# One group of products moved in the forward and in the backward chain of a recurrent attention block

## The chip, the cores and the metric

The kernel runs on one core of one Trainium2 chip. The metric is the device time of one launch in microseconds. The profile names the engines PE (TensorE matmul), PEld (TensorE weight load), DVE (VectorE), ACT (ScalarE), POOL (GpSimd) and SP (SyncE, which issues most of the transfers).

## The reference

The reference computes the output and all gradients of a block that multiplies a memory-augmented attention with a gated unit. The attention walks over 64 segments of 32 tokens. Each segment sees 8 memory rows and its own 32 rows, and its own memory output is the memory of the next segment:

```python
for s in range(n_seg):                       # 64 segments, one after the other
    h = concatenate([mem, xs[s]], axis=1)    # 8 memory rows + 32 rows, width 640
    q, k, v = h @ Wq, h @ Wk, h @ Wv         # 32 heads of 128
    p = softmax(where(mask, q @ k.T * scale, -1e9))
    o = (p @ v) @ Wo
    mem = o[:, :8]                           # feeds the next segment
    outs.append(o[:, 8:])
out = x + s * silu(swiglu(layernorm(x)))     # s: the outs; swiglu with w1, w3, w2
# returned: out and the gradients to x, mem0, Wq, Wk, Wv, Wo, w1, w3, w2
```

Since the memory passes from segment to segment, both the forward pass and the gradient pass hold a chain of 64 steps that can't run side by side.

## The kernel before

The program has five stages one after the other: the gated unit forward, the forward chain (`recurrence`, 390 to 1810 us of the profile with the work around it), the backward chain (`phase4_Abwd`, to 2890 us), the weight gradients of the attention (to 4370 us), and the gated unit backward.

**Chain and fillings.** In each chain, `chain(t, gap)` writes the work of step t that hangs on the memory rows: projections of few rows by `packed_half` (line L306; four column groups of the PE array at a time), a softmax, and output products by `packed_out` (L325). The other 32 rows of a segment don't hang on the chain. Their work is cut into units: three segments (a tile `tl`) by four heads (`qd`), eight units a tile, so three, three and two units a step (`SPL`). At named points the chain calls `gap("W0")`, `gap("W1")`, ..., `gap("G6")`, and what is called there, `at(f, t, i)`, writes operation `f` of unit i of step t into the instruction stream. The order on each engine is the written order (`in_order`): no scheduler moves an instruction of a chain, and each engine works through its list front to back. PE's sum of the chain goes to banks bA, bB, bC of PSUM; the units share five buffers with the tag `x`.

**The fold.** `packed_out` leaves its result in four parts. `fold_add` sums them: ACT copies two parts (`fup`, L334), DVE adds (`fsum`, L336, in two halves). `fold_turn` (L352) then turns the sum on PE, and DVE copies it into the input of the next step (`hx`). Between the last product and the turn PE has only what gaps G4 (backward) or G5 (forward) give it. The table `WARM` names gaps in which PE also gets dummy products of 512 columns whose result nobody reads (L915 forward, L1430 backward).

**Forward unit.** Its scores and softmax run in gaps G1 to G4, `turn_p` (L840) turns the probabilities, `norm` (L831 to L833) normalizes them on POOL and stores them. `pv` forms the value products: `pv_mm` on PE (four products of 96 columns, L860, in the steps that keep them, and four of 128, L863), `pv_turned` copies the first on ACT and stores them from ACT's queue (`xoT`, L872), `pv_rows` copies the second on ACT (`xv`, L92) and stores the rows from POOL's queue (L880). The `pv` of the first unit of step t-1 stands in gap W0 of step t, between the two key halves and the first query half. Key turns of a third unit (`kprep`, L743) stand there too in two of three steps. The first query half goes into bank bA, from which DVE copies the first key half (`stg`, L90).

**Backward unit.** `turn` turns what was loaded, `dprob` (L1337, L1338) forms the gradient of the probabilities, `dsoft` (DVE, L1350 and L1353) that of the scores, and `gmem` forms what the memory rows of keys and values get from the other rows: eight products of 24 columns (L1365, L1366), two copies on ACT (`gks`, L1369), a store from POOL's queue (`GXP`, L1371). `gmem_ld` adds `ld_next`, four loads from SP's queue into the buffer that the products have just read. The step's end is `packed_out` of `gkT` with WkT (48 products), gap G3, `packed_out` of `gqT` with WqT (64 products), `fold_add`, gap G4, `fold_turn`, gap G5. In 59 of the 64 steps, t = 62 to 4, there are units.

Of the kernel before, what the change touches and what calls it, by code (L numbers as in the profile page):

```python
# [554 lines left out]
def recurrence(k, W0, W4, Wv, Wk_, Wq, Wo, own, ps, banks):  # L555
    nc, tc = k.nc, k.tc
    D, DC, S, H, HD, T = k.D, k.DC, k.S, k.H, k.HD, k.T
    with tc.tile_pool(name="achain", bufs=1) as ch, \
# [5 lines left out]
        WARM = dict(G2=1, G3=2, G5=2)  # L564

        def ride_ld(t):
            x0 = k.NB0 + 24 * t
            b, sub = t // 4, t % 4
            if sub == 0 and x0 < S:
                w = min(96, S - x0)  # L570
                rt = ch.tile([P, DC, 96], BF16, name="ride", tag="ride")
                turned_load(k, rt[:, :, 0:w], k.XN[x0:x0 + w, :])
                rides[b] = (rt, w)
# [164 lines left out]
        def kprep(tl, qd, eng='s'):  # L738
            ns, nm, nx, n = k.geo(tl)
            kr = uu.pop(("kr", tl, qd))  # L740
            pt = ps.tile([P, 4, nx], BF16, name="kpt", tag="x", bufs=5)
            for j in range(4):
                nc.tensor.transpose(pt[:, j, :], kr[0:nx, j * P:(j + 1) * P], k.ident[0:nx, 0:nx])  # L743
            dst = kTs[tl % 2][:, qd * 4:qd * 4 + 4, 0:n].rearrange("p h (s c) -> p h s c", c=40)[:, :, :, 8:40]
            k.copy(dst, pt[:].rearrange("p h (s c) -> p h s c", c=32), eng=eng)

        def ld(w, tl, qd, eng=nc.sync):
            nm = k.geo(tl)[1]
            c0 = qd * 512
            r = fl.tile([120, 512], BF16, name=f"x{w}", tag=f"x{w}", bufs=2 if w == "q" else 3)  # L750
            if qd >= (5 if w == "q" else 2):
                ns, nm, nx, n = k.geo(tl)
                g0 = 512 * (qd % 2)
                eng.dma_start(r[nx:n], k.QVM[3 * tl:3 * tl + ns, :, qd // 2, "qv".index(w), g0:g0 + 512].rearrange("t r c -> (t r) c"))
            else:
                k.load_m(r, tl, w, c0, c0 + 512, eng)
            k.load_x(r, 0, k.x_src(tl, w, c0, c0 + 512), eng)
            uu[w, tl, qd] = r
# [84 lines left out]
        def oride_ld(t):  # L843
            if 0 <= t - k.OT0 < k.NO:
                r = ch.tile([P, H, 24], BF16, name="oride", tag="oride")
                nc.sync.dma_start(r[:], k.OTX[t - k.OT0])
                uu["o", t] = r
# [43 lines left out]
        batch = {}  # L891
# [26 lines left out]
        def FILL(g, t, at, kbatch):  # L918
            kb = kbatch.get(t, ())
            if g == "W0":  # L920
                oride_ld(t)
                at(pv, t - 1, 0)
                for u in kbatch.get(t - 1, ())[2:]:
                    kprep(*u)
            elif g == "W1":
                at(pv_mm, t - 1, 1)
                at(pv_turned, t - 1, 1)
                at(turn_p, t - 1, 2)
                at(lambda a, b: ld("v", a, b), t - 1, 2)
            elif g == "V0":  # L930
                at(pv_rows, t - 1, 1)
            elif g == "W2":
                ride_ld(t + 1)
                for u in kb[0:2]:
                    ld_k(*u)
            elif g == "G1":
                oride(t)
                at(pv_mm, t - 1, 2)
                at(turn_q, t, 2)
                for i in range(2):  # L940
                    at(lambda a, b: ld("q", a, b), t + 1, i)
            elif g == "G2":
                at(lambda a, b: pv_turned(a, b, qo=nc.gpsimd), t - 1, 2)
                at(pv_rows, t - 1, 2)
                for i in range(3):
                    at(scores, t, i)
                at(soft_max, t, 0)
                for i in range(2):
                    at(lambda a, b: ld("v", a, b), t, i)
            elif g == "G3":  # L950
                at(lambda a, b: soft_exp(a, b, 0, 2), t, 0)
                at(soft_max, t, 1)
            elif g == "G4":
                at(lambda a, b: soft_exp(a, b, 2, 4), t, 0)
                at(lambda a, b: soft_max(a, b, True), t, 2)
                at(norm, t, 0)
                at(soft_sub, t, 2)
                for u in kb[0:2]:
                    kprep(*u, 'v')
                for u in kb[2:]:  # L960
                    ld_k(*u)
                at(soft_exp, t, 1)
                at(norm, t, 1)
                at(soft_exp, t, 2)
            elif g == "G5":
                at(turn_p, t, 0)
                at(turn_q, t + 1, 0)
                at(turn_q, t + 1, 1)
                at(lambda a, b: ld("q", a, b), t + 1, 2)
            elif g == "G6":  # L970
                at(turn_p, t, 1)
                at(norm, t, 2)
        tail = [u for t in sorted(batch) if t >= T for u in batch[t]]
        fA, fB, fC = [b_[:] for b_ in (bA, bB, bC)]
# [54 lines left out]
        batch = {t: b for t, b in batch.items() if t < T}  # L1029
# [53 lines left out]
def phase4_Abwd(k, out2, W0, W4, WT, own, ps, banks):  # L1083
# [20 lines left out]
    with tc.tile_pool(name="gst", bufs=1) as st, tc.tile_pool(name="gchain", bufs=1) as ch, \  # L1104
# [25 lines left out]
        WARM = dict(G4=1)  # L1130
# [247 lines left out]
        batch = {}  # L1378
# [14 lines left out]
        def gap_of(t):  # L1393
            def at(f, tt, i0, i1=None):
                b = batch.get(tt, ())
                for u in b[i0:i0 + 1 if i1 is None else i1]:
                    f(*u)

            def gap(g):
                if g == "W0":  # L1400
                    ride_ld(t - 1)
                    at(turn, t, 0)
                elif g == "W1":
                    at(turn, t, 1)
                    at(gmem_ld, t + 1, 2)
                elif g == "G1":
                    at(dprob, t, 0)
                elif g == "G2":
                    at(dprob, t, 1)
                    at(turn, t, 2)  # L1410
                    at(dsoft, t, 0)
                elif g == "G3":
                    if t > 0:
                        load_xp(t - 1)
                    at(dsoft, t, 1)
                    at(gmem_ld, t, 0)
                elif g == "G4":
                    at(dprob, t, 2)
                elif g == "G5":
                    at(gmem_ld, t, 1)  # L1420
                elif g == "G6":
                    at(dsoft, t, 2)
                if t == 0 and g == "G1":
                    fetch.append(Fetch(k, W0))
                if t == 0 and g in ("G1", "G2"):
                    fetch[0].to(2 if g == "G1" else 3)
                if t == 0 and g == "G3":
                    fetch[0].w(0)
                for i in range(WARM.get(g, 0)):
                    nc.tensor.matmul((bA if g in ("W1", "G2") else bB)[:], k.ident[:], WqT[:, 0, 0:512], start=True, stop=True)  # L1430
            return gap
        todo = pro + todo
# [859 lines left out]
```

## Time and profile before

| what | value |
|---|---|
| median of 3 runs | 4680.79 us (4674.91 to 4681.3) |
| profiled execution | 4678.86 us, its span 4677.0 us |
| mean granted PE clock | 0.987 |
| PE busy, whole span | 4454.0 us (95%) |
| PEld, DVE, ACT, POOL busy | 2818.5, 2244.2, 1588.7, 2104.2 us |
| forward chain, 390 to 1810 us | PE 1324.05 us busy, clock 0.98, DMA share 0.62 |
| backward chain, 1810 to 2890 us | PE 1030.86 us busy, clock 0.99, DMA share 0.71 |

The span is one execution as the hardware profiler saw it. A row of the order of time gives start, duration, engine, line, operation, what it writes and reads, and in brackets the idle time of the engine ahead of it with what ended it. The busy time of PE counts matmuls whose ends are modelled and overlap, so that the starts of weight loads (PEld) show the pace better. POOL's DMA issues count as its instructions.

### The profile page before, as it was taken

The page shows a single profiled execution, that of the slowest core. Times are in us where ns is not written, and L with a number is a line of the kernel's source. Part 1 is how long each engine was busy: PE and PEld are TensorE (multiplying, and loading weights), DVE is VectorE, ACT ScalarE, POOL GpSimd, SP SyncE. Part 2 cuts the span into 40 slices and gives each one's busy share as a digit, 9 for nine tenths or more (in the row PEclk, how much of TensorE's full clock was granted, in tenths as well). Part 3 has the DMA queues.
Part 4 walks back from the last instruction along what each step waited for, and adds up shares of the span by engine and source line. Part 5 has one row for each costly group of instructions (what it writes and reads, how often), then busy time and mean ns, then how long its engine had stood idle before and what let it go on. Part 6 is the DMA issues. An engine that isn't in the chain of part 4 may idle for free. (4 is left out here: it accounts for less than half of the span.)

```text
span 4677.0 us, 159650 instructions
## 1 busy us (share of the span) xinstructions
PE 4454.0 (95%) x64443; PEld 2818.5 (60%) x64443; DVE 2244.2 (48%) x7156; ACT 1588.7 (34%) x4360; POOL 2104.2 (45%) x3528
## 2 busy tenths in 40 slices
PE   8999999999999888999999998999999999999999
PEld 4544555555555555666666665676667766667675
DVE  8734666666666534555555553343224422311560
ACT  5532555555544533333333332233223322200000
POOL 6532555555555323455444444455335533311440
PEclk9998999999999998999999999999999999999999
DMA  7773565666655677777777775654445543579674
GB/s 259 240 256 119 174 181 176 183 181 183 181 169 170 171 183 224 210 224 210 212 212 212 209 208 153 141 160 135 114 111 157 147 129 109 169 222 209 159 178 101
DMA packets 976843, 834.77 MB, mean 178 GB/s; under 512 B 518890, under 2 KB 858286, under 8 KB 974144
## 3 DMA queue, kind: packets, MB, share of 16 engines
q1 hardware_dynamic: 763879, 547.92, 42.3%
q0 software_dynamic: 129952, 228.13, 16.5%
q10 hardware_dynamic: 82275, 48.52, 3.9%
q8 instruction: 509, 8.34, 0.8%
q14 instruction: 228, 1.87, 0.1%
HBM read 472.66 MB, written 310.33 MB: 167 GB/s over the span
## 5 line engine op out<-in xcount | busy, mean ns | idle before, releaser
L1667 PE MATMUL wg<-gr,hr 128*128 128x512 bf16 x2400 | 521.7, 379 | 0.0
L1648 PE MATMUL g<-land,ghacc 128*128 128x320 bf16 x3072 | 459.5, 300 | 0.8
L1667 PEld LDWEIGHTS <-hr 128*128 128x128 bf16 x2400 | 234.0, 98 | 278.8
L306 PEld LDWEIGHTS <-hx 128*32 128x32 bf16 x10240 | 247.9, 97 | 230.6 <-issue 17.5
L1648 PEld LDWEIGHTS <-ghacc 128*128 128x128 bf16 x3072 | 289.0, 98 | 103.7 <-ACT ghacc L92 2.2
L90 DVE CAST wgo<-wg 128x512 bf16<-128x512 f32 x72 | 49.8, 692 | 471.2 <-PE wg L1667 471.2
L90 DVE CAST stg<-bank 128x512 bf16<-128x512 f32 x256 | 177.1, 692 | 147.3 <-PE bank L306 145.8
L880 POOL DMA_DIRECT2D OR<-xv x163 | 89.9, 552 | 349.9 <-ACT xv L92 320.3
L1613 POOL DMA_DIRECT2D GSP<-grs x48 | 25.6, 543 | 472.6 <-ACT grs L1605 471.7
L92 ACT COPY ghacc<-t6g 128x768 bf16<-128x768 bf16 (+1 forms) x176 | 137.2, 780 | 295.0 <-PE t6g L1630 284.7
L1324 POOL DMA_DIRECT2D VTD<-gvT x176 | 129.6, 741 | 222.1 <-ACT gvT L1323 210.6
L325 PEld LDWEIGHTS <-gkv 128*8 128x8 bf16 x8192 | 177.9, 87 | 80.9 <-DVE gkv L1197 2.7
L812 ACT ACTIVATE xP<-xsp,xnm 120x120 bf16<-120x120 f32 (+1 forms) x540 | 186.6, 373 | 26.6 <-DVE xnm L794 26.6
L832 POOL TENSOR_TENSOR xP<-xP,xrz 120x480 bf16<-120x480 bf16 x163 | 161.4, 990 | 75.3 <-DVE xrz L831 46.3
L1654 DVE TENSOR_TENSOR ghacc<-ghacc,g 128x320 f32<-128x320 f32 x192 | 93.7, 488 | 210.0 <-PE g L1648 210.0
L336 DVE TENSOR_TENSOR fsum<-bank,fup 64x160 bf16<-64x160 f32 x254 | 69.5, 311 | 254.1 <-ACT fup L334 252.5
L92 ACT CAST wgo<-wg 128x512 bf16<-128x512 f32 x48 | 28.1, 586 | 479.8 <-PE wg L1667 413.4
L1371 POOL DMA_DIRECT2D GXP<-gks x157 | 91.1, 580 | 184.9 <-ACT gks L1369 184.1
L325 PE MATMUL bank<-Wo,oTm 128*32 128x320 bf16 x4032 | 154.5, 307 | 18.6 <-DVE oTm L684 18.5
L325 PE MATMUL bank<-WvT,gkv 128*8 128x320 bf16 x4096 | 167.5, 307 | 0.2 <-DVE gkv L1197 0.2
L325 PE MATMUL bank<-WkT,gkv 128*8 128x320 bf16 x4096 | 161.8, 299 | 3.6 <-issue 1.9
L245 POOL DMA_DIRECT2D land<-GOS x256 | 146.7, 579 | 36.5 <-issue 10.2
(389 smaller groups left out, 10896.6 us busy)
## 6 DMA issues: line engine op xcount, KB each, us to landing
QVS<-stg SPq DMA_DIRECT2D x128, 256.0 KB
kT<-VTD SPq DMA_DIRECT2D x64, 320.0 KB
PR<-xP POOLq DMA_DIRECT2D x168, 120.0 KB, 3.2
VTD<-gvT POOLq DMA_DIRECT2D x168, 120.0 KB, 4.0
land<-DSR SPq DMA_DIRECT2D x168, 120.0 KB
land<-PR SPq DMA_DIRECT2D x168, 120.0 KB
OR<-xv POOLq DMA_DIRECT2D x163, 120.0 KB, 3.1
orr<-OR SPq DMA_DIRECT2D x14, 1280.0 KB
```

The lines of the kernel that those rows point to most:

```text
L90: return nc.vector.tensor_copy(out, in_)
L92: return nc.scalar.copy(out, in_)
L245: eng.dma_start(d, src if src.shape[0] > 1 else src[0])
L306: k.nc.tensor.matmul(bank[32 * g:32 * g + 32, :], x[:, dc, :], W[:, dc, c0:c0 + 512], start=(dc == 0), stop=(dc == k.DC - 1), tile_positio ...
L325: k.nc.tensor.matmul(pm[p0:p0 + nq, 0:320], x[:, h, :], W[:, h, 320 * b:320 * b + 320], start=(first and i == 0), stop=(last and i == 15), ...
L812: nc.scalar.activation(Pb[0:n, j, 0:n], sp[0:n, j, :], ACT.Exp, bias=nmx[0:n, j:j + 1], scale=k.scale, accum_out=Z[0:n, j:j + 1])
L832: eng.tensor_tensor(Pb[0:n, :, 0:n], Pb[0:n, :, 0:n], bc_last(rz[0:n], n), ALU.mult)
L1324: nc.gpsimd.dma_start(k.VTD[tl][:, :, h0:h0 + 4, :], vTq[:])
L1371: (nc.sync if (tl, qd) in pro else nc.gpsimd).dma_start(k.GXP[tl, :, qd, 0:ns], ks[:].rearrange("p s i h m -> p s i (h m)"))
L1648: nc.tensor.matmul(pg[:], ring[:, i, j, r0:r0 + P], Ws[qd][i][:, j, 320 * h:320 * h + 320], start=(i == 0 and j == 0), stop=(i == 2 and j ...
L1654: nc.vector.tensor_tensor(a, a, pg[:], ALU.add)
L1667: nc.tensor.matmul(pw[:], hr[:, tl, dc * P:(dc + 1) * P], grs[i][:, tl, :], start=(tl == 0), stop=(tl == NF - 1))
```

## The change

Forward, the `pv` of the first unit leaves gap W0 of the next step and is written in gap G6 of its own step, behind the second unit's `turn_p` and ahead of the third unit's `norm`. Backward, the `gmem_ld` of the first unit leaves gap G3 and is written in gap G4, behind the third unit's `dprob`. In the backward chain the dummy product of G4 is written only in steps without units (t = 63 and t = 3 to 0).

```diff
@@ recurrence, FILL
             if g == "W0":
                 oride_ld(t)
-                at(pv, t - 1, 0)
                 for u in kbatch.get(t - 1, ())[2:]:
                     kprep(*u)
...
             elif g == "G6":
                 at(turn_p, t, 1)
+                at(pv, t, 0)
                 at(norm, t, 2)
@@ phase4_Abwd, gap
                 elif g == "G3":
                     if t > 0:
                         load_xp(t - 1)
                     at(dsoft, t, 1)
-                    at(gmem_ld, t, 0)
                 elif g == "G4":
                     at(dprob, t, 2)
+                    at(gmem_ld, t, 0)
...
-                for i in range(WARM.get(g, 0)):
+                for i in range(0 if batch.get(t) else WARM.get(g, 0)):
                     nc.tensor.matmul((bA if g in ("W1", "G2") else bB)[:], k.ident[:], WqT[:, 0, 0:512], start=True, stop=True)
```

## The prediction

> **What bounds the kernel now.** I read the busy time by stretches first, then the waits of TensorE, then the order of time inside one step of each chain, then the granted clock in stretches of 3.4 us. Two hundred-microsecond rows, one from the forward and one from the backward chain (columns: stretch, length, then busy time and instruction count of PE, PEld, DVE, ACT, POOL, then granted clock, DMA share, GB/s):
>
> ```profile
> 1000.00:1100.00 100.00, 96.48 (x1879) 58.86 (x1872) 65.23 (x182) 52.33 (x168) 56.76 (x88) 1.00 0.61 182
> 2500.00:2600.00 100.00, 96.47 (x2282) 63.84 (x2274) 54.11 (x279) 34.23 (x115) 48.05 (x88) 1.00 0.72 210
> ```
>
> PE is busy for 96% in both and no other engine passes 67%. Both chains are one serial line of PE work with small holes. The reader is to see that a product moved from one place of PE's list to another gains only where it leaves a place in which PE has no hole and lands in one. The largest holes of each chain, from the waits of PE (total us, times, longest), forward first, backward second:
>
> ```profile
> PE bank L325 <- DVE oTm L684: 18.3, 58, 0.4
> ...
> PE bank L352 <- DVE fsum L336: 24.0, 62, 0.6
> ```
>
> So the backward fold wait is the one large hole of its chain (62 steps). One backward step in order of time (start, duration, engine, line, idle time before it in brackets):
>
> ```profile
> 2315.62 0.10 PEld L1430 LDWEIGHTS <-ident 128*128 128x128 bf16 x1 [0.27 <-issue]
> 2315.63 0.39 PE L1430 MATMUL bank<-WqT,ident 128*128 128x512 bf16 x1
> 2315.75 0.42 ACT L334 COPY fup<-bank 64x320 f32<-64x320 f32 x1 [1.88 <-PE bank L325]
> 2316.20 0.55 DVE L336 TENSOR_TENSOR fsum<-bank,fup 64x160 bf16<-64x160 f32 x2 [2.50 <-ACT fup L334]
> 2316.57 0.78 PE L352 MATMUL bank<-sel,fsum 64*128 64x8 bf16 x6 [0.56 <-DVE fsum L336]
> ...
> 2328.34 1.46 PEld L325 LDWEIGHTS <-gkv 128*8 128x8 bf16 x48
> ...
> 2330.08 0.10 PEld L1365 LDWEIGHTS <-kT 120*128 120x128 bf16 x1 [0.28 <-DVE xPT L1353]
> ...
> 2330.37 2.00 PEld L325 LDWEIGHTS <-gqT 128*8 128x8 bf16 x64
> ```
>
> The first five lines are the fold wait: the last product of the step ends near 2315.7, ACT copies, DVE adds, and the turn (L352) starts 0.95 us after the dummy product (L1430) was started. The last three are the place the memory-row products (L1365/L1366) stand in today: between the key products (48, from 2328.34) and the query products (64, from 2330.37), where PE has no lack of work.
>
> **The change, backward.** The eight memory-row products of the step's first unit leave gap G3 and go into the fold wait (G4), behind dprob of the third unit where there is one; in steps that have units the dummy product is gone. 59 steps (t = 62 to 4) have units.
>
> Leaving G3: the block holds PE from 2330.08 to 2330.37, 0.29. It also splits one stream of 112 equal products in two. Blocks of this stream take 0.78 (20), 1.60 (44), 1.755 (48) and 2.28 (64) from their start to the next start: 0.034 each and 0.10 to 0.12 per block for leaving it. One block less: 0.11. Together 0.40 us a step. The query products need gqT from ACT: its two copies start at 2328.45 and take 0.45, so it is ready near 2328.9, 1.1 us before the earlier start. The gap is not a cover for anything.
>
> Arriving in the fold wait: 0.95 us are there from the end of the step's products to the turn, which DVE's sum ends. Without a third unit the eight products take about 0.3 of them, with one 0.25 + 0.3. The turn starts no later; at least 0.35 us stay free. The dummy (one 512-column product, 0.39) made way. Cost nothing, covered by ACT's 0.42 and DVE's first half. If the cover were gone the 0.3 would be back. ACT's two gks copies (0.39) now stand behind fup instead of ahead of it; ACT has nothing until 2320.17, so nobody waits. Their store on POOL's queue moves from 2331.4 to some 3 us later, behind the same DSR store and ahead of the same GXP and GWO stores: the order of POOL's queue is the same. SP's four loads for the next unit wait for these products and start about 2.9 us later; SP's order is unchanged too. SP is busy 10 to 15 of a 17 us step; in the fullest steps all behind them (the loads L1151 to L1167) slips by some 0.7 us (four loads of 2.3 us that now meet the second unit's four). L1151 is issued up to 3 us after its buffer comes free already, and about 12 us before its reader. Hidden, except where DMA is already late: from one turn L352 to the next, single steps take 17.95, 18.95 and 20.81 against a regular 17.02, 17.02, 16.64. I allow 0 to +5 us, and some luck the other way; value taken 0.
>
> Backward sum: 59 x 0.40 = 23.6 us.
>
> **The change, forward.** The first unit's value products (four 96-wide L860, four 128-wide L863) move from between key and query projection (W0) to the step's end (G6), ahead of the next key projection.
>
> ```profile
> 1002.56 0.39 PE L840 MATMUL xpp<-ident,xP 120*128 120x120 bf16 x4
> 1002.67 0.20 DVE L699 CAST hx<-bank 128x40 bf16<-128x40 f32 x1 [0.33 <-PE bank L352]
> ...
> 1002.92 1.85 PEld L306 LDWEIGHTS <-hx 128*32 128x32 bf16 x40
> ...
> 1004.24 0.69 DVE L90 CAST stg<-bank 128x512 bf16<-128x512 f32 x1 [0.85 <-PE bank L306]
> 1005.19 0.20 PEld L860 LDWEIGHTS <-xv 120*128 120x128 bf16 x4 [0.42 <-issue]
> ...
> 1005.34 0.25 PEld L863 LDWEIGHTS <-xPT 120*128 120x128 bf16 x4
> ...
> 1005.69 0.77 PEld L306 LDWEIGHTS <-hx 128*32 128x32 bf16 x20
> ```
>
> At G6 there is no hole worth the name: the key projection starts at 1002.92, 0.36 after the four turns, which is what four turns and the change of tile shape cost elsewhere (1027.46 to 1027.82), and hx comes at 2.87. So the products cost their full 0.35 there (0.14 + 0.21, to the next 128-wide start). At W0 they give back the same 0.35 in steps in which key turns (L743) follow them (1023.76 to 1024.11): 40 steps, net 0. In the 20 steps without (t = 6, 9, ... 63) they give 0.50 (1005.19 to 1005.69) and the key and query streams join: a block of 20 takes 1.19, one of 40 2.27, so one leaving of 0.11. 0.61 - 0.35 = 0.26: 20 x 0.25 = 5 us. This needs bank A free when the query products reach it: DVE's copy runs from 1004.24 to 1004.93, the key products end near 1005.2. 0.2 us to spare, the thinnest margin of the sum; if it is used up the gain is 0 to 5.
>
> ACT is idle 3.08 us before its copy of these products and takes xoT, its issue and xv there 2 us earlier. POOL's queue does change: the store of the rows (L880), which waits for ACT, comes ahead of the third unit's normalization. By the durations above it is issued about 2.6 us after the turns, 0.54 long, so the normalization (0.99) runs from 3.1 to 4.1 instead of 1.8 to 2.8, and its reader (L840 in W1) comes at 6.3: hidden with 1.9 to spare. The value loads are issued about 7 us before G6; hidden.
>
> **The rule on the clock.** The row first: in the steps without units (t = 3 to 0), the stretch 2858.60 to 2862.01 had PE busy 2.49 of 3.41 us, at full clock, and the next had half.
>
> ```profile
> 2858.60:2862.01 3.41, 2.49 (x53) 1.49 (x42) 1.26 (x5) 0.59 (x1) 0.00 (x0) 1.00 0.20 77
> 2862.01:2865.43 3.42, 3.42 (x59) 1.74 (x59) 1.45 (x7) 0.37 (x1) 0.00 (x0) 0.50 0.40 114
> 2568.07:2571.49 3.42, 2.72 (x59) 1.63 (x51) 0.75 (x3) 0.74 (x3) 0.80 (x2) 1.00 0.67 182
> ```
>
> The Trainium skill ("TensorE: Matmul & The Clock Gate", Part 1) has the clock halved only after a whole idle window of about 3.4 us. By it a hole of 0.56 is harmless, the dummy was worth nothing, and the sum is 28.6. By the row 73% busy is already too little, and the third line, a fold wait with a dummy, stands at 80%. Then the dummy may matter. I follow the row and still take 0: eight products end where the dummy ended (0.2 of starts and 0.17 for the last, against 0.39), so the busy share stays near 80%. Only if the gate counts columns (512 before, 8 x 24 now) does it fall.
>
> **The sum.** 23.6 + 5 = 28.6 off the profiled execution of 4678.86 (span 4677.0): 4650.3. The median before, 4680.79, is 1.9 above that execution, so I forecast 4651.
>
> **Rivals.**
> 1. Backward only: bank A or POOL's new order eats the forward gain, or late DMAs take some of it: 23.6 less 0 to 10, so 4656 to 4666. For it: the 0.2 us margin, and seven waits of the turns for POOL (7.2 us) today. Against: all other queues have 1 us or more.
> 2. Half clock after fold waits, the one that ends slower. Steps without units, turn to turn, took 15.85 without a halved stretch and 17.23 and 17.00 with one: 1.15 to 1.4 each. At one a step, 59 x 1.25 = 74: 4651 + 74 = 4725. It decides from 23 halvings on (28.6 / 1.25). For it: the 73% row. Against: backward windows that hold turns and small products only already run with few columns and kept 1.00.
> 3. The products are no shorter in sum: the step's end is set by DMA or SP and 0.40 comes back as a wait, 4675 to 4682. For it: DMA share 0.72, SP 15 of 17 us. Against: PE waits for a DMA only in single steps, and step times repeat as 17.02, 17.02, 16.64.
>
> **Numbers.** 0.2% (about 9.4 us, what a measurement of this kernel can tell from no change) puts the border at 4671.4. Forecast 0.70 (4643 to 4657), rival 1 0.17, rival 2 0.06 (0.05 of it above 4690), rival 3 0.07. Faster 0.87, same 0.08, slower 0.05. The range takes in rival 1: 4641 to 4669.
>
> **What would show it.** Right: backward steps of 16.62, 16.62 and 16.24 instead of 17.02, 17.02 and 16.64; one stream of 112 products; the turn's wait for DVE about as long as now; forward steps shorter by 0.25 every third time; clock 1.00 through both chains. Wrong: halved stretches at the fold waits, PE waits at L306 for DVE's copy of bank A, at L840 for POOL, or at L1226, L1262, L1320 for loads.

## The result, and the profile after

The changed kernel took 4666.7 us (median of 8 runs, 4663.12 to 4675.85), the kernel before beside it 4679.57 (8 runs, 4668.41 to 4682.73): ratio 0.998, 95% interval 0.997 to 0.9989. That is 12.9 us less, where 28.6 less had been forecast. The profiled execution has a span of 4665.3 us (4677.0 before) and a mean granted clock of 0.984 (0.987 before).

The two stretches of 100 us look nearly as before, but the second no longer has a clock of 1.00:

```profile
1000.00:1100.00 100.00, 95.27 (x1908) 59.82 (x1914) 66.78 (x185) 53.82 (x168) 55.73 (x86) 1.00 0.62 182
2500.00:2600.00 100.00, 95.31 (x2278) 64.28 (x2278) 54.12 (x281) 33.94 (x114) 47.59 (x87) 0.98 0.74 209
```

One backward step in order of time shows that the change does what it says. The query products (64) follow the key products (48) with nothing between; the eight memory-row products stand in the fold wait, and the turn (L352) still starts when DVE's sum lets it:

```profile
2305.42 1.46 PEld L325 LDWEIGHTS <-gkv 128*8 128x8 bf16 x48
...
2306.91 2.13 PEld L325 LDWEIGHTS <-gqT 128*8 128x8 bf16 x64
...
2309.32 0.10 PEld L1365 LDWEIGHTS <-kT 120*128 120x128 bf16 x1 [0.28 <-issue]
...
2309.45 0.42 ACT L334 COPY fup<-bank 64x320 f32<-64x320 f32 x1 [3.48 <-PE bank L325]
...
2309.90 0.55 DVE L336 TENSOR_TENSOR fsum<-bank,fup 64x160 bf16<-64x160 f32 x2 [2.09 <-ACT fup L334]
...
2310.28 0.78 PE L352 MATMUL bank<-sel,fsum 64*128 64x8 bf16 x6 [0.59 <-DVE fsum L336]
```

In a forward step without key turns, the value products (L860, L863) stand between the turns and the key projection, and key and query projection are one stream of 60 weight loads:

```profile
996.20 0.24 PEld L860 LDWEIGHTS <-xv 120*128 120x128 bf16 x4
...
996.38 0.25 PEld L863 LDWEIGHTS <-xPT 120*128 120x128 bf16 x4
...
996.73 2.93 PEld L306 LDWEIGHTS <-hx 128*32 128x32 bf16 x60
```

Measured from turn to turn, the difference of the spans (11.7 us) is made up like this:

| stretch of the profile | before, us | after, us | difference |
|---|---|---|---|
| start to first forward turn | 392.1 | 390.9 | -1.2 |
| forward turns, first to last | 1166.8 | 1158.1 | -8.7 |
| last forward turn to first backward turn | 259.0 | 263.5 | +4.5 |
| backward turns, first to last | 1055.1 | 1048.1 | -7.0 |
| rest | 1803.9 | 1804.6 | +0.7 |

The 4.5 us lie within the scatter: over all 20 profiles of this study, the stretch from the last forward turn to the first transposes of the backward took 161 to 166 us with the old forward part (8 profiles, mean 163.5) and 162 to 167 with the new (12, mean 164.5). Of the 8.7 us in the second row some is luck too; over all profiles the mean difference is 4.0. The row to explain is the fourth. The regular backward steps became 16.63, 16.25 and 16.62 us (17.02, 16.64 and 17.02 before), which is the forecast to a hundredth. But I call "excess" what the steps take above the regular step of their kind (the median of the twelve shortest of about twenty), summed over the chain: it went from 9.1 to 25.7 us. 23.6 us were taken off and 16.6 came back.

Where they came back is in the waits of PE in the backward chain (total us, times, longest):

```profile
PE bank L352 <- DVE fsum L336: 26.6, 62, 0.9
PE gvpt L1320 <- DMA kT<-QVS: 6.9, 5, 1.9
...
PE ggpt L1327 <- DMA kT<-GOS: 0.9, 2, 0.5
```

The last two lines are new in size: transposes of a unit wait for the loads of its rows. Before, the first of them stood at 1.6 us, once:

```profile
PE gvpt L1320 <- DMA kT<-QVS: 1.6, 1, 1.6
```

The reason is in SP's queue. First a step of the kernel before, then one of the kernel after (L1307 is the first of the four loads of a unit, L265 with QVS the second, L352 the turn):

```profile
2138.91 0.57 SPq L1174 DMA_DIRECT2D xp<-GXP  x1
2139.58 0.61 SPq L1307 DMA_DIRECT2D kT<-QVM  x1
2140.24 0.61 SPq L265 DMA_DIRECT2D kT<-QVS  x1
...
2140.59 0.78 PE L352 MATMUL bank<-sel,fsum 64*128 64x8 bf16 x6 [0.29 <-DVE fsum L336]
```

```profile
2129.56 1.19 SPq L1174 DMA_DIRECT2D xp<-GXP  x1
...
2130.76 0.78 PE L352 MATMUL bank<-sel,fsum 64*128 64x8 bf16 x6 [0.31 <-DVE fsum L336]
2130.85 0.56 SPq L1307 DMA_DIRECT2D kT<-QVM  x1
2131.46 0.61 SPq L265 DMA_DIRECT2D kT<-QVS  x1
...
2136.83 0.51 PE L1320 MATMUL gvpt<-ident,kT 120*128 120x120 bf16 x4 [1.57 <-DMA kT<-QVS]
```

Before, the load left 1.0 us ahead of the turn, now 0.1 behind it. There are four load buffers, so the load that is issued when the first unit's products have read their buffer is for the fourth unit from there. In a step with three units (39 of 58) that is the second unit of the very next step, whose transposes stand in W1; in a step with two units it is the third unit of the next step, whose transposes come later, in G2. In the 39 steps that count the load left 2.89 us ahead of the turn before and 0.30 after, and its reader came 7.24 us behind the issue before and 4.65 after (medians; the issue is that of L1307, the first of the four loads).

In 34 of the 39 steps 4.65 us were enough, but for one wait of 0.2 us. In the other five the reader waited by more than half a microsecond and started 4.5 to 6.2 us after the issue, so that is how long the rows can take. In these five SP had fallen behind: the load left 0.1 to 0.5 us behind the turn. So the change took away the slack that had hidden a late SP. The kernel before shows the same thing once: its only wait stands in the one step of the 39 in which the load left 0.24 us ahead of the turn; in the other 38 it left 1.0 us or more ahead. Over the eleven profiles of this study with four buffers and with SP's order and the reader in their old places (429 such loads), 38 of the 45 loads that left less than 0.25 us ahead of the turn were waited for by more than 0.3 us, 9 of the 202 that left 0.25 to 0.35 ahead, and 1 of the 182 that left earlier.

The Trainium skill ("DMA: Bandwidth & Descriptors", "Anatomy of one DMA — SWDGE (gpsimd) path") prices a transfer that GpSimd issues at about 2.0 us and its bytes at 436 GB/s. This load is issued by SP, which that section doesn't price. Taken over all the same, it makes an estimate of 2.5 us for the 192 KB of QVS, in good time for a lead of 4.65. The row above has 5.4 us from the issue of QVS at 2131.46 to the reader, with the transfer engines 0.69 busy (the share in the stretch shown next). The measured figure decides: with it the waits are expected, with the estimate they are not.

A wait costs more than its own length, because of what the clock does behind it. Stretches of 3.41 us around that wait:

```profile
2133.50:2136.91 3.41, 1.79 (x34) 0.98 (x27) 1.18 (x4) 1.57 (x4) 3.19 (x7) 1.00 0.69 208
2136.91:2140.32 3.41, 3.41 (x64) 2.88 (x67) 0.71 (x2) 1.75 (x6) 1.31 (x2) 0.50 0.68 225
2140.32:2143.74 3.42, 3.42 (x54) 1.58 (x54) 1.32 (x6) 0.00 (x0) 0.00 (x0) 0.50 0.91 300
```

The stretch with the wait has PE busy for 1.79 of 3.41 us, and the next two have half the clock: this step took 4.2 us too long for 1.57 us of wait. Over the chain, half clock went from 10.2 to 27.3 us. A stretch at half clock does half its work, so 17.1 us more of it are up to 8.5 us lost; with 6.8 us more of waits for loads (1.6 to 8.4, over all the rows of a unit) that is 15.3 of the 16.6 us.

### The profile page after: what moved, and what is told of

Read it like the earlier page. It is cut to its first block, busy times and chain, and to the rows that moved or that the text cites. A ratio compares the mean times of both kernels' runs of the same rounds, so it can differ in the third digit from the quotient of the medians.

```text
span 4665.3 us, 159314 instructions
## 1 busy us (share of the span) xinstructions
PE 4404.6 (94%) x64162; PEld 2830.3 (61%) x64384; DVE 2243.2 (48%) x7156; ACT 1593.2 (34%) x4360; POOL 2105.6 (45%) x3528
## 3 DMA queue, kind: packets, MB, share of 16 engines
q0 software_dynamic: 129952, 228.13, 16.6%
q14 instruction: 228, 1.87, 0.1%
## 5 line engine op out<-in xcount | busy, mean ns | idle before, releaser
L306 PEld LDWEIGHTS <-hx 128*32 128x32 bf16 x10240 | 251.2, 96 | 228.0 <-issue 16.0
L90 DVE CAST wgo<-wg 128x512 bf16<-128x512 f32 x72 | 49.8, 692 | 471.2 <-PE wg L1667 471.2
L245 POOL DMA_DIRECT2D land<-GOS x256 | 147.0, 580 | 38.3 <-PE r6p L1598 10.3
```

The lines of the kernel that those rows point to most:

```text
L90: return nc.vector.tensor_copy(out, in_)
L245: eng.dma_start(d, src if src.shape[0] > 1 else src[0])
L306: k.nc.tensor.matmul(bank[32 * g:32 * g + 32, :], x[:, dc, :], W[:, dc, c0:c0 + 512], start=(dc == 0), stop=(dc == k.DC - 1), tile_positio ...
```

## Experiments

All ratios are to the kernel before, run beside each group on the same chip. Its median was 4685.56, 4686.9, 4686.88, 4685.37 and 4681.96 us in the five groups, so only times of one group are compared. "Excess" is defined above; "load waits" is the sum of PE's waits for a unit's loaded rows, both from the profiled run.

| run | group | median us | ratio (95%) | excess us | load waits us |
|---|---|---|---|---|---|
| fwd_only | 1 | 4687.39 | 1.0002 (0.9993 to 1.0012) | 12.0 | 2.5 |
| bwd_only | 1 | 4688.33 | 1.0 (0.9989 to 1.0012) | 29.1 | 6.9 |
| a_5buf | 1 | 4667.38 | 0.9964 (0.9951 to 0.9978) | 20.5 | 0 |
| b_5buf | 1 | 4697.57 | 1.0027 (1.0017 to 1.0037) | 14.1 | 0 |
| a_again | 2 | 4675.86 | 0.998 (0.997 to 0.9991) | 34.2 | 12.2 |
| a_end | 2 | 4674.51 | 0.9971 (0.996 to 0.9982) | 25.1 | 6.5 |
| b_end | 2 | 4680.34 | 0.9985 (0.9976 to 0.9994) | 3.8 | 1.1 |
| a_dummy | 2 | 4673.15 | 0.9964 (0.995 to 0.9977) | 33.0 | 10.3 |
| b_late | 3 | 4691.71 | 1.001 (0.9997 to 1.0024) | 20.5 | 5.6 |
| a_swap | 3 | 4671.96 | 0.9969 (0.9957 to 0.9981) | 26.8 | 6.1 |
| a_xpfirst | 3 | 4673.6 | 0.9974 (0.9962 to 0.9987) | 33.6 | 5.3 |
| a_end_5buf | 3 | 4667.66 | 0.9964 (0.9953 to 0.9975) | 16.9 | 0 |
| a_turn2 | 4 | 4697.94 | 1.0028 (1.0015 to 1.0041) | 18.8 | 0 |
| b_turn2 | 4 | 4735.15 | 1.0098 (1.0084 to 1.0112) | 25.8 | 0 |
| a_k1 | 4 | 4681.0 | 0.9989 (0.9979 to 0.9999) | 40.0 | 13.6 |
| b_k1 | 4 | 4688.01 | 1.0004 (0.9992 to 1.0017) | 17.6 | 4.7 |
| a_best | 5 | 4659.26 | 0.9947 (0.9933 to 0.9961) | 16.2 | 2.6 |
| b_best | 5 | 4685.14 | 1.0 (0.9989 to 1.0011) | 5.2 | 0 |

**The two halves alone.** fwd_only is the changed kernel with the backward edits undone, bwd_only with the forward edit undone.

> Only the forward part of the change (value products at the step's end; the backward is that of before, dummy product included). Theory L (late loads): the forward part is whole, and what was lost was lost in the backward. The forward steps from the first to the last fold turn take 1158 us as in the changed kernel (1166.8 before), the backward steps 1055 us as before (59 steps of 17.02, 17.02 and 16.64 us), so 4669 to 4673 us (ratio 0.9975 to 0.9985). Theory C (the clock: the waits in the backward open because the dummy product is gone and TensorE falls to half clock): the same for this kernel, since its dummy products are there. Theory N (the lost time is scatter of the backward, whatever is in it): the backward has an excess over its regular steps that may be 25 us here too, and the total may then be as high as 4685.

> Only the backward part of the change (memory-row products after the third unit's scores, dummy product gone, loads issued later; the forward is that of before). Theory L: regular backward steps of 16.63, 16.63 and 16.25 us, but an excess over them of about 25 us against 9 before, in steps where TensorE waits for the rows of the second unit (transposes at L1320 and L1327); the 59 steps take 1046 to 1050 us, the forward 1167 us, the total 4671 to 4677 us. Theory C: the same total. Theory N: the excess may be 9 here, and the total then 4656 to 4660.

Neither could be told from the kernel before by its time, and both took longer than any total expected of them (4687.39 against 4685 at most, 4688.33 against 4677 at most). Why stays open: alone the halves gain nothing, together they gave 0.998 twice. The profiles, one execution each, tell more: the backward of bwd_only has regular steps of 16.63, 16.41 and 16.62 us and an excess of 29.1; that of fwd_only has 17.02, 16.65 and 17.02 and 12.0. Where the backward is the changed one the excess is large (25.7, 34.2 and 29.1 in three profiles), where it is not it is small (9.1 and 12.0). That speaks against theory N, as far as single profiles can.

**The changed kernel again.** a_again is the same kernel in a later group.

> The changed kernel itself once more, on the same chip and beside the same runs of before as the three below. So far: changed 0.998 [0.997, 0.9989] of before, forward part alone 1.0002 [0.9993, 1.0012], backward part alone 1.0 [0.9989, 1.0012]. Theory L+C2 (the change takes 8 us off the forward steps and 6 to 7 us off the backward ones, and the rest of the span scatters by some 5 us from run to run): ratio 0.996 to 0.999, an excess of the backward steps of 20 to 30 us with 20 us or more of it made of waits and of stretches at half clock. Theory N (the changed kernel isn't faster at all, its first result was a good draw): ratio 0.9995 to 1.001.

The ratio repeats, 0.998; this profile has even more waits for loads and 37.5 us at half clock.

**Late loads alone, without the rest.** Six of the first unit's eight products stay where they were and two go into the fold wait, so that the buffer comes free late (part 1 of `gmem` is the products of three heads, part 2 those of the fourth and the copies):

```diff
                 elif g == "G3":
...
-                    at(gmem_ld, t, 0)
+                    at(lambda a, b: gmem(a, b, 1), t, 0)
                 elif g == "G4":
                     at(dprob, t, 2)
+                    at(lambda a, b: gmem_ld(a, b, 2), t, 0)
```

> The kernel before, with the late loads alone: of the first unit's eight memory-row products six stay where they were (ahead of the query fold) and two go behind the third unit's scores in the wait for the fold, so that the unit's buffer comes free, and the loads into it leave, as late as in the changed kernel. Dummy product and forward are those of before. Theory L (late loads are what ate the backward's gain): regular steps shorter by the two products, 16.92, 16.92 and 16.54 us (6 us over 59 steps), and an excess of 20 to 35 us where before had 9 and this chip's two other kernels with the old backward 12 to 15; waits of L1320 for QVS of 5 us or more with half clock behind them; total 5 to 20 us over before (ratio 1.001 to 1.004). Rival P (it is the place of the products itself, or the clock, that makes the excess): excess as before, total 4 to 8 us under before (0.9982 to 0.9992).

The loads left 0.44 us ahead of the turn (median). The regular steps saved less than forecast (16.97, 16.72 and 16.97 us), and the excess is 20.5 us, with the wait that belongs to it:

```profile
PE gvpt L1320 <- DMA kT<-QVS: 5.3, 4, 2.3
```

The time is 4.8 us over before, at the lower edge of what was expected, and the interval still holds 1. So waits for loads appear though the dummy product and most of the products are where they were (5.6 us against 1.6). They are not all of this excess: of the 17.1 us at half clock in the steps with units, 6.8 stand behind waits for loads and 10.2 behind waits of 1.75 and 1.99 us that the profile puts down to "issue" (explained at the end).

**A fifth load buffer.** The load behind a unit is then for the fifth unit from there, no longer the fourth, so every load goes out one unit earlier. The buffer is one of the two for the k rows:

```diff
-            kr = krbs[t % 2][0:104]
+            kr = krbs[1][0:104]
...
-            g = i % 6 if early else (i - len(pro) + 1) % NG
+            g = i % 6 if early else (1, 2, 3, 0, 4)[(i - len(pro)) % 5]
...
+        ld_next()
         load_k(T - 1)
```

> The changed kernel with a fifth buffer for the loads of the backward: the unit loaded when the first unit's products are done is then the third unit of the next step, not the second, and every load is issued one unit earlier than it is needed now. The fifth buffer is one of the two k-row buffers of the memory rows; these rows use the other one alone, so that their load starts only when the step's own products have read it. Theory L: the excess of the backward steps falls from 25.7 us to 10 or less, the waits of L1320 for QVS and of L1327 for GOS to under 3 us, the stretches at half clock that follow such waits go with them, and the total is 4645 to 4655 us. Theory C: the half clock comes from the missing dummy product and not from the loads, so the waits move but the excess stays over 20 us: 4661 to 4670 us. Theory Q (the k-row load, now later, becomes the new wait): 4665 or more, with waits of the query products at L1261 or thereabouts for KS.

> Control: the kernel before with the same fifth buffer. Theory L: before had 9.1 us of excess, of which some 3 us are waits of L1320 for loads and a stretch at half clock of 6.8 us; so 4671 to 4679 us, 0 to 9 us under before. If this kernel gains as much as the changed one does from the fifth buffer, the buffer's gain is not the delay that the change brought. Theory C: no change (4677 to 4682). Theory Q: slower than before.

Every wait for a unit's rows is gone in both kernels, and the changed one stands 4697.57 - 4667.38 = 30.2 us under the other. But 12.0 of these are a control that became slower than the kernel before; against the kernel before itself it is 18.2. Theory L's total was missed: the excess stays at 20.5, with 8.7 us of waits that the profile puts down to "issue". The largest row of these waits, first in the changed kernel, then in the control:

```profile
PE bank L325 <- issue: 7.9, 13, 1.8
```

```profile
PE bank L325 <- issue: 7.6, 9, 2.1
```

Besides, two stretches of the changed kernel run at half clock (t = 15 and 12) with no wait for a load ahead of them. The stretch ahead of the second, and that one itself:

```profile
2658.07:2661.48 3.41, 2.57 (x53) 1.62 (x47) 0.75 (x3) 0.82 (x4) 1.05 (x2) 1.00 0.64 145
2661.48:2664.90 3.42, 3.38 (x33) 1.47 (x37) 0.69 (x1) 0.39 (x2) 2.36 (x5) 0.50 0.94 267
```

The first of these rows holds the fold wait (0.57 us) and no other pause over 0.2. The same was seen once more, in a_xpfirst (1894.79). So half clock followed a stretch whose longest pause was the fold wait in 3 of the 649 steps with units in the eleven profiles without the dummy product, at up to 1.7 us each, and in none of the nine profiles with it. Whether the dummy would have prevented them was not tested with the loads in time.

Since the fifth buffer costs a k-row buffer, that cost was tested by itself, with the four load buffers as they were (only the first hunk above):

> The changed kernel with one buffer for the k rows in place of two and the four load buffers as they were: the fifth buffer's price alone. If the price is that of a later k-row load, which holds up SP's queue (with xp, the late loads and the store behind it), the excess is 5 to 15 us over the changed kernel's 25 to 35, total 4680 to 4692 (0.9985 to 1.001). If it costs nothing: 0.998 as the changed kernel.

> The kernel before with one buffer for the k rows. The kernel before with the fifth buffer was 12 us slower than before (1.0027). If the price of the single k-row buffer made that: 1.002 to 1.004 here. If it was the fifth buffer's earlier loads: 0.9995 to 1.0005.

One k-row buffer costs the kernel before next to nothing (1.0004) and the changed one some 4 us (0.9989 in place of 0.998), within the intervals. With it and four load buffers the change is worth 4688.01 - 4681.0 = 7.0 us, with it and five 30.2. So it is not the k rows that make the difference, but the loads: by the ratios they took 11.7 us off the changed kernel (0.9989 to 0.9964), and its excess fell from 40.0 to 20.5. Why the same buffer made the kernel before about 11 us slower than b_k1 (1.0027 against 1.0004) is not settled; its "issue" waits are 7.6 us against 2.9.

**The readers later, in place of the loads earlier.**

```diff
                 elif g == "W1":
-                    at(turn, t, 1)
                     at(gmem_ld, t + 1, 2)
-                elif g == "G1":
                     at(dprob, t, 0)
+                elif g == "G1":
+                    at(turn, t, 1)
```

> The changed kernel with the readers of the late load moved later: in W1 the step before's third unit's products and then the first unit's scores, and the second unit's transposes only in G1, some 2.5 to 3 us later, where the scores were. Buffers as in the changed kernel. Theory L: the longest wait of L1320 for QVS in three profiles of the changed kernel's kind was 2.7 us, so nearly all such waits go, with the half clock behind them: excess 8 to 16 us (against 25 and 35), total 4655 to 4667 us where before has 4687 (0.993 to 0.9957). If the late loads were not the cause (theory K: the fifth buffer's effect was something else), the excess stays at 25 to 35 us and the ratio at 0.997 to 0.999. Rival W: the first unit's scores wait in W1 for ACT's copies of its transposes, new waits of 0.2 to 0.5 us a step at L1337 make regular steps longer by that, 10 to 25 us in all, and eat the gain.

> Control: the kernel before with the same exchange. Theory L: its loads left 2.4 us earlier and were in time but for a few steps, so 0 to 8 us under before (0.998 to 1.0), and the changed kernel with the exchange stands 20 to 30 us under this one. Rival W: slower than before by 10 to 25 us, as the changed one is slowed.

Rival W came true: the scores wait for ACT 0.6 us in every step, the same in both kernels (this line is the changed one's), and both are slower.

```profile
PE gdp L1337 <- ACT xqT L1329: 35.2, 59, 0.7
```

But no row of a unit is waited for, and the changed kernel stands 37.2 us under the other: 59 steps of 0.40 again (17.24 against 17.64), the forward part, and half clock of 34 us against 58, up to 12 us. The control fell to half clock in 15 steps behind its waits for ACT, the changed kernel in 7, so this part is not the change's gain from its products.

**The dummy product.** The changed kernel with the line of the dummy product as it was:

> The changed kernel with the dummy product in the wait for the fold kept in every step, beside the products that the change put there. Theory C (the half clock comes from the missing dummy product): the 27 us at half clock in the backward fall to about the 10 of before, the excess to 13 to 17 us, and the total is 5 to 10 us under the changed kernel's. Theory L/D (the half clock follows the waits for loads): the half clock stays at 17 to 30 us and the total is the changed kernel's or up to 13 us more (59 products of 0.21 us, if they don't hide in the wait that the moved products have left).

The regular steps stay (16.63, 16.33 and 16.62), so it hides in what the products leave of the fold wait. Half clock in the chain is 34 us and the excess 33, and the wait for QVS is as large as ever:

```profile
PE gvpt L1320 <- DMA kT<-QVS: 9.6, 5, 3.7
```

So the missing dummy is not the cause of the half clock behind the waits for loads. The time, 0.9964 of 5 runs, can't be told from the changed kernel's 0.998.

**What else is on the transfer queues.** 17 of the 25 us of excess lay between the turn of step 53 and that of step 37, and at the ends of steps 53 to 38 POOL also issues 16 copies, some of them large. In a_end and b_end they go out in steps 6 to 0:

```diff
-            if later and t < T - 10:
+            for _ in range(0 if t > 6 else min(len(later), 1 if t > 4 else 3)):
                 nc.gpsimd.dma_start(*later.pop(0))
```

> The changed kernel with the 16 copies that a line of the backward's loop issues on POOL in steps t = 53 to 38 (two of a part of the turned weights, twelve of memory rows into HRO, two of 840 KB into SR) issued in steps t = 6 to 0 instead, behind the last loads of units. 17 of the 25 us of excess in the changed kernel lie in those 16 steps. Theory D (the copies crowd the transfer queues, so that the now later loads of the second unit come after their reader, and TensorE's own instructions come late): the excess in steps 53 to 38 falls from 17 to under 5 us, the waits of L1320 for QVS to under 2.5 us, and the total is 4652 to 4660 us where the changed kernel gives 4670 (ratio to before 0.994 to 0.9965). Theory L alone (the loads are late by their own place in SP's order, whatever else is in flight): the waits spread over other steps, the excess stays over 18 us and the total equals the changed kernel's. Theory E (the copies cost at the end what they cost in the middle): excess moves to t = 6 to 0 or to the first 30 us after the backward; total equal.

> Control: the kernel before with the copies moved to the same steps t = 6 to 0. Its excess was 9 us, of which 8 lay in t = 53 to 38. Theory D: the loads leave 2.4 us earlier here and are in time almost always, so there is less to gain: 2 to 8 us (ratio 0.9985 to 0.9995); the difference between this kernel and the changed one with the copies moved is the change without its late loads, 20 to 29 us. Theory L alone: no change (0.9995 to 1.0005). If both gain the same, the copies are a cost of their own and not what ate the change's gain.

Theory D fell for the changed kernel: its waits stayed (t = 43, 31 and 19) or came in other steps (t = 55 and 28), and the excess stays at 25.1. The kernel before gained 6.6 us, and its excess went to 3.8: without the copies its loads are in time almost always. The changed kernel's are sometimes late without the copies too.

**Small means.** a_swap exchanges the two pieces of W1, so that the reader comes 0.4 us later; a_xpfirst moves the 256 KB load that SP issues ahead of the late ones.

> The changed kernel with two pieces in the wait of W1 exchanged: the products of the step before's third unit (0.40 us) now stand ahead of the transposes of the second unit, so that the reader of the late load comes 0.4 us later. Theory L: waits of L1320 that were under 0.4 us go, longer ones are shorter by 0.4 us, and some of the half clock behind them goes; excess 17 to 27 us where the changed kernel's two profiles had 25 and 35; total 3 to 9 us under the changed kernel's (ratio to before 0.996 to 0.9975). If the loads were late by chance and not by a fixed margin: no change (0.998).

> The changed kernel with the 256 KB load of xp, which SP issues directly ahead of the late loads, moved ahead of the load of the k rows (some 3 us earlier in the step). Theory L with contention (the late loads land late because they share the transfer engines with xp): the loads land 0.5 to 1.5 us sooner, the excess falls to 10 to 20 us, total 8 to 15 us under the changed kernel's (0.995 to 0.9965). Theory L without it (issue time alone decides): waits as in the changed kernel, total equal (0.9975 to 0.9985). Rival: the k-row loads, now behind xp, come late for the query products at L1262: new waits there, total over the changed kernel's.

Neither is told from the changed kernel by its time. In a_swap four waits of 1.3 to 1.5 us stay. In a_xpfirst the waits for loads fell (from 8.4 and 12.2 to 5.3 us), but "issue" waits rose to 9.9, and the excess is as large as ever.

**Together.** First the fifth buffer and the moved copies; then the exchange, the moved copies, and the QVS rows issued by ACT (`nc.sync if early else nc.scalar` in `ld`), with the same three for the kernel before.

> The changed kernel with the fifth buffer and with the 16 copies issued in steps 6 to 0. The fifth buffer alone took away every wait of L1320 for a load, but its profile had 8 us of waits in which nothing that the profile shows is missing (before products of L325, up to 1.8 us each), most of them in steps 53 to 38; moving the copies took such waits from the kernel before, whose excess fell to 5 us. Theory L+D: both causes are gone here: excess 5 to 12 us, backward steps 1030 to 1038 us, total 4655 to 4662 us on this chip, where before has 4686 (ratio 0.993 to 0.995). If the 8 us are the k-row load's doing (it leaves later with one buffer): excess 15 to 25 us, total like the fifth buffer's alone (0.996 to 0.9975).

> The changed kernel with three small things for the late load: the two pieces of W1 exchanged (reader 0.4 us later), the QVS rows of the late units issued by ACT instead of as second of four on SP (0.5 us or more sooner), and the 16 copies in steps 6 to 0. Theory L: waits of L1320 for QVS fall from 7 us to 3 or less; excess 12 to 20 us; total 4660 to 4668 us where before has 4686 (0.9945 to 0.9962). If ACT's issue costs the evictions behind it as much as it brings: 0.997, as with the exchange or the copies alone.

> Control: the kernel before with the same three. The copies alone gave it 0.9985. Theory L: its loads were in time nearly always, so the other two bring nothing: 0.998 to 0.999, and the changed kernel stands 12 to 22 us under it. If the means help this one as much as the changed one, its loads were late as well and the change's loss had another cause.

a_end_5buf is no faster than the fifth buffer alone; theory L+D expected 0.993 to 0.995. Of its excess of 16.9 us, 8.1 are waits for "issue" and up to 3.4 half clock in the steps with units. a_best is the fastest kernel of this study, 0.9947, with 2.6 us of waits for loads left, and it stands 25.9 us under b_best, which the same three didn't help at all, and 22.7 under the kernel before. So between kernels with the same arrangement the change is worth 26 to 37 us where the loads are in time (30.2, 37.2 and 25.9), and 6 to 13 where they are not (12.9 at first, 11.0 in group 2, 7.0 and 5.8).

That is not all the change's own. Two of the three controls were made slower than the kernel before, b_5buf by 12.0 us and b_turn2 by 49.8. And in the profiles, one execution each, the backward turns from first to last took 14.8 us less in a_5buf than in b_5buf and 12.8 less in a_best than in b_best, where 23.6 had been forecast: the regular steps are shorter by the 0.4 us, but the excess is still 6.4 and 11.0 us larger. Late loads are shown as a cause of the loss, not as the whole of it.

## Why the prediction was wrong

- **Leaving G3, 0.40 a step: right.** 0.39, 0.39 and 0.40, in all profiles with the changed backward but one kind of step of three (16.25 to 16.41).
- **Arriving in the fold wait at no cost: right.** The idle time ahead of the turn is 0.31 and 0.59 us where it was 0.29 and 0.56, and a_dummy shows that even the dummy product would still fit.
- **"SP's four loads for the next unit wait for these products and start about 2.9 us later ... Hidden": this is the step that failed.** The delay was named, and 0 to +5 us allowed. Its size was about right: 2.6 us in the median of the 39 loads that are read in the very next W1, and 1.9 over all 58, since SP was often held up by its own queue before. But the step looked at what stands behind these loads on SP (L1151 and on, 12 us ahead of their reader) and not at the reader of the loads themselves, which comes 4.65 us after them. The value taken was 0; the excess grew by 16.6 us in the first profile, of which waits for loads and the half clock behind them make up to 15.3, and by 25.1 in the second. The profile of before had the sign: one wait of L1320 for QVS, 1.6 us long, in the one step whose load left as late as nearly all leave now.
- **Clock, valued 0: nearly right for the dummy, wrong in sum.** In the changed kernel's own profile the fold waits didn't lower the clock (in other profiles without the dummy they did, three times in all). The waits for loads did, five times in the first profile, and up to half of what came back is that.
- **Forward, 20 x 0.25 = 5 us: right in the chain's own time, not seen in the run times.** Every third step is 0.27 shorter (18.45 to 18.18, later 18.10 to 17.84), the others 0.05. From first to last turn, the 12 profiles with the new forward take 1160.9 us in the mean, the 8 with the old 1165.0: 4.0 us. No wait for bank A at L306 showed, and L840 waited for POOL 1.7 us in the first profile and 3.6 to 4.3 in the others with the new forward, 3.3 to 4.0 with the old: no new wait. In the run times this gain does not show: fwd_only stands at 1.0002, with an interval from 0.9993.
- **The rivals.** The median lies inside the stated range of 4641 to 4669, but with 12.9 us of the 28.6. It ended just beyond rival 1 (4656 to 4666), by its second cause, late DMAs, which it had at 0 to 10 us. Rival 2 had half clock, but it came behind load waits and in a few steps; behind fold waits it came three times in all the profiles. Rival 3's sign, step times that no longer repeat, appeared in a tenth of the steps.

## What to carry to other kernels

When work is moved that frees a buffer, find the reader of what is loaded into that buffer and compare the new lead with the time the load takes on a busy machine, from the late cases of the trace; an operation that is free on its own engine can be dear by what it releases. Look at the steps in which the issuing queue runs late, not only at the regular one: here 0.3 us ahead of the turn were enough in 34 steps of 39, and the other five made most of the loss. A wait can cost more than its length: waits of 1.4 to 1.9 us made their steps 3.0 to 4.8 us too long, because the clock dropped behind them. And when a gain fails to show, test the change on a version in which the suspected wait is impossible, beside a control with the same arrangement, and look at what the arrangement does to the control: here the control itself became 12 us slower, so that the difference between the two says less than it seems to.

## What the runs showed of the hardware that was not expected

**The clock does not go by PE's busy time alone.** In the stretch 2133.50 of the changed kernel PE was busy 1.79 of 3.41 us and the clock was halved. In a_5buf a stretch with less, 1.57 of 3.41, was followed by full clock:

```profile
2231.40:2234.81 3.41, 1.57 (x48) 0.88 (x36) 1.77 (x12) 0.63 (x3) 0.00 (x0) 1.00 0.69 211
2234.81:2238.22 3.41, 2.99 (x79) 1.82 (x73) 0.00 (x0) 0.98 (x4) 3.13 (x6) 1.00 0.58 174
```

The first was filled with projections up to 2134.25 and then transposes of 120 columns, this one with 320-column products of `packed_out`. But the stretches that held such products fell too when they held less: 1.34 us in a_xpfirst (below) and 1.42 in b_late (2562.92).

```profile
2130.31:2133.72 3.41, 1.34 (x42) 0.79 (x36) 0.36 (x2) 0.00 (x0) 2.16 (x5) 1.00 0.94 231
2133.72:2137.14 3.42, 3.30 (x55) 1.87 (x43) 0.54 (x2) 0.66 (x3) 0.00 (x0) 0.50 0.27 80
```

What of the work counts was not tested, and the busy time is modelled. The Trainium skill ("TensorE: Matmul & The Clock Gate", Part 1) has the clock at half after an idle window of about 3.4 us; here it fell after stretches that were half busy.

**PE can stop in the middle of a stream with no wait that the profile shows.** In a_end_5buf:

```profile
1931.64 1.11 PE L325 MATMUL bank<-WqT,gqT 128*8 128x320 bf16 x25
1934.63 1.53 PE L325 MATMUL bank<-WqT,gqT 128*8 128x320 bf16 x39 [1.87 <-issue]
```

One stream of 64 products stands still for 1.87 us. In the transfers of 1932.0 to 1933.4 the trace has one packet on the queue marked "instruction", which runs from 1932.12 to 1933.33:

```profile
q8 instruction: 1, 0.02, 5.4%
```

All ten stops of this kind above 0.3 us in that kernel's backward chain ended 2.2 to 3.0 us after the start of such a packet. Over all 20 profiles it is 108 of 114 such stops, and none ended sooner behind a packet, while the time from 2.2 to 3.0 us behind a packet makes up 14% of a chain. That fits instructions that arrive late on busy queues. It was not tested by itself. These waits came to 0.7 to 9.9 us a chain over the kernels. In a_5buf, with the loads in time, they and the half clock in the steps with units make 12.1 of the 20.5 us of excess; the rest was not traced.
